# The order of a fused spectral-filter and expert kernel: x turned ahead of the previous tile's second product, a rank product timed by VectorE's count, and later landing times for loads

## The chip, the cores and the metric

The kernel runs on one core of one Trainium2 chip. The metric is the device time of one execution in microseconds (us); the time before is 1613.07 us, the median of three runs (1609.99 to 1613.96). PE is TensorE, DVE is VectorE, ACT is ScalarE, POOL is GpSimd, SP is SyncE, whose queue issues the direct DMAs.

## What is computed

The input x is (8, 2496, 256), all data float32. Each of the 8 batches is filtered along its sequence, and the filtered tokens then go through a mixture of 8 experts, one expert per token:

```python
X = np.fft.rfft(x, axis=1)
y = np.fft.irfft(X * (filt_r + 1j * filt_i), n=2496, axis=1)   # per batch and channel
x = y.reshape(19968, 256)
logits = x @ w_gate                                            # 8 experts
expert = argmax(logits); gate = softmax(logits)[expert]
out[token] = gate * (relu(x[token] @ w1[expert]) @ w2[expert]) # hidden width 1024
```

## The kernel before

**Two halves, one instruction stream.** The filter half takes the transform of length 2496 as 39 x 64: four matrix products a batch, called stages a, b, c and d, with the result of a stored in DRAM (zd) and read again for b, and that of c stored (ud) and read again for d. Stage b also multiplies by the filter on DVE (lines 358 to 362). After stage d the tokens are transposed (turn_y), the logits formed, and `route` ranks the tokens of each expert and scatters them to a list in DRAM with indirect DMAs on POOL (line 606). `tile_map` then works out, on rows of 8 to some 160 numbers, which expert and which row of the list each tile takes (lines 625 to 676).

The expert half works through that list in tiles of 512, 256 and, at the end, 128 rows. One tile i has these parts:

- `turn_x` (T below): 8 transposes for a 512-row tile on PE (line 736), copies to xT, copies of the token numbers and gates to idt and gts on DVE (lines 730, 731; three buffers), and four subtractions on POOL that form `sums` (lines 742 to 745);
- two `half`s (H): the product with w1, the hidden width split in two. Tiles of 512 rows and 256-row tiles of the last batch save one product in eight by combining quarters (`hidden_by_quarters`): seven products in all, each four matmuls in the profile; the third product is the first to need `sums`. Each also needs `wsum`, four sums over the weights on POOL (lines 752 to 755). DVE adds the parts (line 779), ACT copies and applies relu (lines 788, 783). Other tiles use `hidden` (line 816);
- `result` once per 128 rows (R, four for a 512-row tile): 16 matmuls in the profile with w2 (line 833), scaling by the gate to ys on ACT or DVE (lines 837, 838), and an indirect DMA on POOL that writes the 128 rows of the output (line 839).

**What sets the order.** The program is written out at build time by a planner: the loop at the end of the kernel keeps a modelled clock `now`, and takes either the next filter step (`STEPS`) or the next expert step (the generator `experts`). The order on PE, DVE, ACT and SP is that of the program; on POOL the framework chooses it. The planner's rules that the change touches:

- `more_loads` issues the filter half's loads and writes their modelled landing to `lands`. If the next filter step's load counts as not yet landed (`late_in`), an expert step may go first even without credit.
- `prefetch` does the same for x and the weights of the expert half; `due` asks whether their modelled landing is past.
- `side` runs the steps of `route` and `tile_map`, up to four between two planner steps. For each bare `yield` it adds 0.3 us to `free["v"]`, the planner's count of when DVE is free. `either` uses `free["v"]` to place a copy on DVE or ACT. A `yield "wait"` costs one of the four calls and nothing else.
- In `route` sixteen such waits, thus about four planner steps, stand between the one-hot tile `oe` (line 526, DVE) and the rank products that read it (lines 537, 538, PE).
- `experts` orders a tile's parts. In the steady state, with everything due, the order on PE is ... R(i-1), T(i+1), H(2i+1), H(2i+2), R(i), T(i+2) ...: the next tile's first half already stands ahead of the last tile's second product, and T stands behind it.

Of the kernel before, what the change touches and what calls it, by code (L numbers as in the profile page):

```python
# [118 lines left out]
def kernel(  # L119
# [92 lines left out]
    now = [0.0]  # L212
    free = {"v": 0.0, "s": 0.0, "p": 0.0}
# [284 lines left out]
    def route(b, g):  # L498
        t0 = 8 * g
        w = min(8, NG - t0)  # L500
        lg = lgs[b][:, t0:t0 + w]
        sh3 = (TP, w, E)
        she = (TP, E, w)

        def small(name, *shape, dt=F32, tag=None, rows=TP):
            n = int(np.prod(shape))
            full = sb.tile([rows, 8 * n // w if w in shape else n], dt, tag=tag or name, name=name, bufs=1)[:, :n]
            return full.rearrange("p (a b) -> p a b", a=shape[0]) if len(shape) == 2 else full

        mx = small("mx", w)  # L510
        nc.vector.tensor_reduce(mx, lg, axis=AX.X, op=ALU.max)
        oh = small("oh", w, E)
        ex = small("ex", w, E)
        nc.vector.tensor_tensor(oh, lg, mx[:, :, None].to_broadcast(sh3), op=ALU.is_ge)
        yield
        nc.vector.tensor_tensor(ex, lg, mx[:, :, None].to_broadcast(sh3), op=ALU.subtract)
        nc.scalar.activation(ex, ex, AF.Exp)
        nc.vector.tensor_tensor(oh, oh, em8[:TP, None, :].to_broadcast(sh3), op=ALU.mult)
        yield
        idx = small("idx", w)  # L520
        nc.vector.tensor_reduce(idx, oh, axis=AX.X, op=ALU.min)

        nc.vector.tensor_tensor(idx, idx, vld[:, t0:t0 + w], op=ALU.mult)
        yield
        oe = small("oe", E, w)
        nc.vector.tensor_tensor(
            oe, idx[:, None, :].to_broadcast(she), em8[:TP, :, None].to_broadcast(she), op=ALU.is_equal
        )
        sd = small("sd", w)
        nc.vector.tensor_reduce(sd, ex, axis=AX.X, op=ALU.add)  # L530
        yield

        for _ in range(16):
            yield "wait"
        rk = psr.tile([P, 2, E * NG], F32, tag="rk", name="rk")
        oef = oe.rearrange("p e t -> p (e t)")
        mm(rk[:TP, 0, :E * w], lhsT=tri, rhs=oef, start=True, stop=True)
        mm(rk[:, 1, :E * w], lhsT=ones, rhs=oef, start=True, stop=True)
        rks = sb.tile([P, 2, 8 * E], F32, tag="rks", name="rks", bufs=1)
        nc.vector.tensor_copy(rks[:TP, 0, :E * w], rk[:TP, 0, :E * w])  # L540
        nc.vector.tensor_copy(rks[:, 1, :E * w], rk[:, 1, :E * w])
        nc.vector.tensor_scalar(sd, in0=sd, scalar1=1e-9, scalar2=None, op0=ALU.add)
        nc.vector.reciprocal(sd, sd)
        yield
        yos = [outs.pop(("o", b, c)) for c in range(2 * g, min(2 * g + 2, len(CH)))]
        for c, yo in enumerate(yos):
            n = min(4, w - 4 * c)
            sh8 = (TP, n, 8)
            nc.vector.tensor_scalar(
                yo.bitcast(I32)[:, :n, D:D + 8], in0=ids0[:, t0 + 4 * c:t0 + 4 * c + n, None].to_broadcast(sh8),  # L550
                scalar1=float(b * S), scalar2=None, op0=ALU.add,
            )
            nc.vector.tensor_copy(yo[:, :n, D + 8:], sd[:, 4 * c:4 * c + n, None].to_broadcast(sh8))
            yield
        run = small("run", E, w, rows=P)
        runf = run.rearrange("p e t -> p (e t)")
        nc.vector.tensor_tensor_scan(
            runf, segs[w], rks[:, 1, :E * w], 0.0, op0=ALU.mult, op1=ALU.add
        )
        yield  # L560

        pos = small("pos", E, w)
        posf = pos.rearrange("p e t -> p (e t)")
        nc.vector.tensor_tensor(posf, runf[:TP], rks[:TP, 1, :E * w], op=ALU.subtract)
        nc.vector.tensor_tensor(posf, posf, rks[:TP, 0, :E * w], op=ALU.add)
        yield
        bs = sb.tile([TP, E], F32, tag="bs", name="bs", bufs=1)
        nc.vector.tensor_tensor(bs, cnt[:TP], eoff[:TP], op=ALU.add)
        nc.vector.tensor_tensor(pos, pos, bs[:, :, None].to_broadcast(she), op=ALU.add)
        yield  # L570
        nc.vector.tensor_tensor(pos, pos, oe, op=ALU.mult)
        rowf = small("rowf", w)
        nc.vector.tensor_reduce(rowf, pos.rearrange("p e t -> p t e"), axis=AX.X, op=ALU.add)
        yield
        row = sb.tile([TP, 8], U32, tag="row", name="row", bufs=2)[:, :w]
        nc.vector.tensor_copy(row, rowf)
        nc.vector.tensor_tensor(cnt, cnt, run[:, :, w - 1], op=ALU.add)
        yield
        rows = []
        for t in range(w):  # L580
            m = N1 if t0 + t == NG - 1 else TP
            rows.append((row[:m, t:t + 1], yos[t // 4][:m, t % 4, :]))
        pool(now[0] + 2.0, 0)
        for at, what in rows:
            scatter(b, at, what)
            yield "pool"
        held_y[0] -= len(yos)
        if t0 + w == NG:
            rows_at[b] = free["p"] + 4.0
# [30 lines left out]
    def tile_map(b, rows, n, last):  # L620
# [6 lines left out]
        nc.vector.tensor_scalar(  # L627
            av_i, in0=av_i, scalar1=rows.bit_length() - 1, scalar2=None, op0=ALU.arith_shift_right
        )
        yield  # L630
        nc.vector.tensor_copy(av, av_i)
        nc.vector.tensor_tensor_scan(end, one, av, 0.0, op0=ALU.mult, op1=ALU.add)

        base = pools["moe"].tile([1, E], F32, name="base", bufs=1)
        add = pools["moe"].tile([1, E], F32, name="add", bufs=1)
        nc.vector.tensor_tensor(base, done, eoff[0:1, :], op=ALU.add)
        yield
        nc.vector.tensor_scalar(add, in0=av, scalar1=-float(rows), scalar2=None, op0=ALU.mult)
        nc.vector.tensor_tensor(add, add, base, op=ALU.subtract)
        nc.vector.tensor_tensor(add[:, :E - 1], add[:, :E - 1], base[:, 1:], op=ALU.add)  # L640
        yield
        most = max(m for group in GROUPS for _, m in group)
        tau = pools["moe"].tile([1, most], F32, tag="tau", name="tau", bufs=1)[:, :n]
        past = pools["moe"].tile([1, most, E - 1], F32, tag="past", name="past", bufs=1)[:, :n]
# [1 line left out]
        nc.vector.tensor_tensor(  # L646
            past, tau0[:, :n, None].to_broadcast(she), end[:, None, :E - 1].to_broadcast(she), op=ALU.is_ge
        )
        yield
        ef = pools["moe"].tile([1, most], F32, tag="ef", name="ef", bufs=1)[:, :n]  # L650
        erow = pools["moe"].tile([1, n], I32, tag=f"erow{n}", name="erow", bufs=2)
        nc.vector.tensor_reduce(ef, past, axis=AX.X, op=ALU.add)
        nc.vector.tensor_copy(erow, ef)
        nc.vector.tensor_tensor(past, past, add[:, None, :E - 1].to_broadcast(she), op=ALU.mult)
        yield
        rf = pools["moe"].tile([1, most], F32, tag="rf", name="rf", bufs=1)[:, :n]
        rrow = pools["moe"].tile([1, n], I32, tag=f"rrow{n}", name="rrow", bufs=2)
        nc.vector.tensor_reduce(rf, past, axis=AX.X, op=ALU.add)
# [6 lines left out]
            nc.vector.tensor_scalar(rrow, in0=rf, scalar1=stop[:, 0:1], scalar2=None, op0=ALU.min)  # L665
        else:
            nc.vector.tensor_copy(rrow, rf)
        yield
        if not last:

            take = pools["moe"].tile([1, E], F32, name="take", bufs=1)
            nc.vector.tensor_tensor(take, av, end, op=ALU.subtract)
            nc.vector.tensor_scalar(take, in0=take, scalar1=float(n), scalar2=0.0, op0=ALU.add, op1=ALU.max)
            nc.vector.tensor_tensor(take, take, av, op=ALU.min)
            nc.vector.tensor_scalar(take, in0=take, scalar1=float(rows), scalar2=None, op0=ALU.mult)
            nc.vector.tensor_tensor(done, done, take, op=ALU.add)
            yield
        work.extend((rows // P, erow[0:1, i:i + 1], rrow[0:1, i:i + 1], b) for i in range(n))


# [232 lines left out]
    def more_loads():  # L913

        while todo and len(ins) < NIN:
            kind, b, c = todo[0]
            if kind != "x" and ({"z": "a", "u": "c"}[kind], b) not in stored:
                return
            todo.pop(0)
            {"x": load_x, "z": load_z, "u": load_u}[kind](b, c)  # L920
            lands[kind, b, c] = now[0] + 6.0

    def after(b):
        for rows, n in GROUPS[b]:
# [5 lines left out]
    def side():  # L930

        while sides and not (held[0] == "pool" and free["p"] > now[0] + 1.5):
            try:
                held[0] = next(sides[0])

                free["v"] = max(free["v"], now[0]) + (0.3 if held[0] is None else 0.0)
                return
            except StopIteration:
                sides.pop(0)
                held[0] = None  # L940
# [24 lines left out]
    def experts():  # L965
# [4 lines left out]
        def turned(i):  # L970
            if used["x"] == i:
                yield lambda: turn_x(i), 0.22 * TILES[i][0], ("x", i)
                used["x"] += 1
# [19 lines left out]
        def due(what, i):  # L993
            return when.get((what, i), now[0] + 1.0) <= now[0]

        for i in range(NT):
            yield from turned(i)
            if used["w1"] == 2 * i:
                yield from half(2 * i)
            if due("x", i + 1):  # L1000
                yield from turned(i + 1)
            yield from half(2 * i + 1)
            if used["x"] == i + 2 and due("w1", 2 * i + 2):
                yield from half(2 * i + 2)
            for j in range(TILES[i][0]):
                yield lambda: result(i, j), 3.42, ("w2", 2 * i + 1)
            hs.pop(i), idt.pop(i), gts.pop(i), w2t.pop(2 * i, None), w2t.pop(2 * i + 1, None)
            used["w2"] += 2

    def share():  # L1010

# [74 lines left out]
```

## Time and profile before

| | |
|---|---|
| time, median of 3 | 1613.07 us |
| span of the profiled execution | 1615.9 us |
| PE busy | 1530.9 us, 95% of the span, 7624 matmuls |
| DVE busy | 753.2 us, 47% |
| ACT busy | 519.6 us, 32% |
| POOL busy | 671.9 us, 42% |
| matmuls with w2 in the 4- and 2-block tiles (line 833) | 500.7 us, 2240 of them, 381 ns each by the profile |
| DMA | 287.54 MB, 178 GB/s over the span |
| mean granted PE clock | 0.979 |

Reading it: PE's spans overlap, since a matmul starts before the one ahead of it has ended; sixteen matmuls of 128x256 that the profile gives as 381 ns each take 3.45 us in a row. PE's idle time is what counts here, and the list of PE's waits gives it by the instruction that waited and what it waited for. From 1100 us on only the expert half is left; before that the two halves are mixed; the first 200 us have little or no expert work to mix in.

### The profile page before, as it was taken

The page shows a single profiled execution, that of the slowest core. Times are in us where ns is not written, and L with a number is a line of the kernel's source. Part 1 is how long each engine was busy: PE and PEld are TensorE (multiplying, and loading weights), DVE is VectorE, ACT ScalarE, POOL GpSimd, SP SyncE. Part 2 cuts the span into 40 slices and gives each one's busy share as a digit, 9 for nine tenths or more (in the row PEclk, how much of TensorE's full clock was granted, in tenths as well). Part 3 has the DMA queues.
Part 4 walks back from the last instruction along what each step waited for, and adds up shares of the span by engine and source line. Part 5 has one row for each costly group of instructions (what it writes and reads, how often), then busy time and mean ns, then how long its engine had stood idle before and what let it go on. Part 6 is the DMA issues. An engine that isn't in the chain of part 4 may idle for free. (4 is left out here: it accounts for less than half of the span.)

```text
span 1615.9 us, 24022 instructions
## 1 busy us (share of the span) xinstructions
PE 1530.9 (95%) x7624; PEld 1213.0 (75%) x7624; DVE 753.2 (47%) x1938; ACT 519.6 (32%) x1059; POOL 671.9 (42%) x817
## 2 busy tenths in 40 slices
PE   7989877999999999999999898999998999999998
PEld 6534546677678778886788687787887888999997
DVE  4677664344755664356555354365342334420000
ACT  4434332333333233222333232223231222233433
POOL 4132224314534644354445545554445446631111
PEclk9999998999999999999999999999999999999999
DMA  8679866697865494356544623352343547676561
GB/s 240 170 201 297 270 215 222 210 279 226 245 203 179 146 283 144 99 160 174 165 128 127 193 93 118 111 156 92 117 161 137 165 133 253 191 240 177 173 188 36
DMA packets 119280, 287.54 MB, mean 178 GB/s; under 512 B 17587, under 2 KB 58812, under 8 KB 119157
## 3 DMA queue, kind: packets, MB, share of 16 engines
q1 hardware_dynamic: 99941, 242.69, 50.0%
q0 software_dynamic: 19216, 43.33, 7.8%
q8 instruction: 62, 1.02, 0.3%
q14 instruction: 61, 0.50, 0.1%
HBM read 205.95 MB, written 80.90 MB: 178 GB/s over the span
## 5 line engine op out<-in xcount | busy, mean ns | idle before, releaser
L833 PE MATMUL bank<-w2t,hT 128*128 128x256 f32 x2240 | 500.7, 381 | 0.0
L833 PEld LDWEIGHTS bank<-w2t,hT 128*128 128x128 f32 x2240 | 424.8, 191 | 73.3 <-issue 16.7
L839 POOL DMA_INDIRECT out_dram<-ys,idt x163 | 163.0, 1000 | 551.9 <-ACT ys L838 205.9
L779 DVE TENSOR_TENSOR hT<-bank,hT 128x512 f32<-128x512 f32 (+1 forms) x504 | 299.3, 627 | 147.0 <-PE bank L775 65.2
L606 POOL DMA_INDIRECT rows<-yo,row x176 | 174.7, 993 | 197.9 <-issue 63.2
L783 ACT ACTIVATE hT<-hT 128x1024 f32<-128x1024 f32 (+1 forms) x144 | 132.4, 956 | 337.7 <-DVE hT L779 330.9
L775 PE MATMUL bank<-sums,wsum 128*128 128x256 f32 (+1 forms) x864 | 189.6, 367 | 28.8 <-POOL sums L743 18.3
L838 ACT ACTIVATE ys<-bank,gts 128x256 f32<-128x256 f32 x160 | 75.7, 473 | 409.9 <-PE bank L833 333.1
L775 PEld LDWEIGHTS bank<-sums,wsum 128*128 128x128 f32 x864 | 152.6, 195 | 61.0 <-POOL sums L743 20.5
L227 DVE COPY xT<-bank 128x128 f32<-128x128 f32 (+2 forms) x55 | 25.9, 471 | 308.1 <-PE bank L736 267.8
L816 PE MATMUL bank<-xT,w1t 128*128 128x128 f32 (+1 forms) x928 | 132.9, 298 | 0.0
L816 PEld LDWEIGHTS bank<-xT,w1t 128*128 128x128 f32 x928 | 120.3, 192 | 11.5 <-issue 5.9
L775 PE MATMUL bank<-xT,w1t 128*128 128x256 f32 (+1 forms) x576 | 123.8, 358 | 0.6 <-ACT hT L788 0.4
L775 PEld LDWEIGHTS bank<-xT,w1t 128*128 128x128 f32 x576 | 99.0, 191 | 15.4 <-issue 3.0
L752 POOL TENSOR_TENSOR wsum<-w1t 128x256 f32<-128x256 f32 x73 | 53.9, 738 | 112.2 <-PE bank L775 97.6
L358 DVE TENSOR_TENSOR ys<-bank,ht 128x512 f32<-128x512 f32 x80 | 54.9, 687 | 86.3 <-PE bank L351 60.4
L372 PE MATMUL bank<-ys,tcs 128*128 128x512 f32 x140 | 74.9, 617 | 12.4 <-DVE ys L362 7.9
L822 ACT ACTIVATE hT<-bank 128x128 f32<-128x128 f32 (+1 forms) x229 | 67.9, 299 | 57.2 <-PE bank L816 45.4
L833 PE MATMUL bank<-w2s,hT 128*128 x368 | 83.2, 379 | 0.0
L391 PE MATMUL bank<-fin,tds 120*117 120x512 f32 x140 | 68.2, 608 | 8.3 <-DMA fin<-ud 7.4
L337 PE MATMUL bank<-fin,tas 117*120 117x512 f32 x154 | 75.5, 609 | 0.0
L351 PE MATMUL bank<-fin,tbs 128*128 128x512 f32 x140 | 75.0, 619 | 0.1
(149 smaller groups left out, 1757.9 us busy)
## 6 DMA issues: line engine op xcount, KB each, us to landing
w1t<-in_moe_w_dram SPq DMA_DIRECT2D x130, 512.0 KB
w2t<-in_moe_w_dram SPq DMA_DIRECT2D x84, 512.0 KB
fin<-in_x_dram SPq DMA_DIRECT2D x40, 512.0 KB
fin<-zd SPq DMA_DIRECT2D x70, 256.0 KB
ud<-uo SPq DMA_DIRECT2D x70, 256.0 KB
zd<-zo SPq DMA_DIRECT2D x35, 480.0 KB
fin<-ud SPq DMA_DIRECT2D x35, 480.0 KB
xg<-rows SPq DMA_DIRECT2D x28, 544.0 KB
```

Source lines behind the costliest of these rows:

```text
L337: mm(p[:TK, :], lhsT=tas, rhs=xt[:TP, j:j + 2, :], start=True, stop=True)
L351: mm(p, lhsT=tbs, rhs=zi[:, j:j + 2, :], start=True, stop=True)
L372: mm(p, lhsT=tcs, rhs=ys, start=True, stop=True)
L391: mm(p[:TP, :], lhsT=tds, rhs=ui[:TK, j:j + 2, :], start=True, stop=True)
L606: sc = nc.gpsimd.indirect_dma_start(out=rowsd, out_offset=bass.IndirectOffsetOnAxis(ap=at, axis=0), in_=what, in_offset=None,)
L775: mm(q[:, v], lhsT=left[:, v * P:(v + 1) * P], rhs=right, start=True, stop=True)
L779: nc.vector.tensor_tensor(o, q, a, op=ALU.add)
L783: nc.scalar.activation(o.rearrange("p v r c -> p v (r c)"), q.rearrange("p v r c -> p v (r c)"), AF.Relu)
L816: mm(p[:, :m], lhsT=w1t[2 * i + g][:, dh, fh, v * P:(v + 1) * P], rhs=xts[i][:, dh, :m], start=(dh == 0), stop=(dh == DH - 1))
L833: mm(p[:, :D], lhsT=hs[i][k % 4 // 2][:, k // 4, k % 2, j * P:(j + 1) * P], rhs=w2, start=(k == 0), stop=(k == FT - 1))
L838: lambda: nc.scalar.activation(ys, p[:, :D], AF.Copy, scale=gate))
L839: nc.gpsimd.indirect_dma_start(out=out, out_offset=bass.IndirectOffsetOnAxis(ap=idt[i].bitcast(U32)[:, j, :], axis=0), in_=ys, in_offset=None,
```

## The change

Four edits to the planner; the arithmetic stays as it is.

1. `experts`: T of the tile after next stands ahead of R, so that the order becomes ... H(2i), T(i+1), R(i-1), H(2i+1), H(2i+2), T(i+2), R(i) ... It is meant to give POOL the time of R to form `sums`. If w1 or x of the next tile isn't due, R goes first as before.
2. `route`: in place of the sixteen waits, the rank products wait until the modelled clock has passed the planner's count of VectorE plus 1.0 us.
3. `route` and `tile_map`: each yield carries a number, and `free["v"]` grows by 0.15 us times that number rather than by 0.3 us. Most numbers are 2; others are 1, 3, 4 and 5.
4. `more_loads`: loads count as landed 10 rather than 6 us after their issue.

```diff
@@ route
-        yield
+        yield 2
 ...
-        for _ in range(16):
+        due = free["v"] + 1.0
+        while now[0] < due:
             yield "wait"
         rk = psr.tile([P, 2, E * NG], F32, tag="rk", name="rk")
 ...
         nc.vector.reciprocal(sd, sd)
-        yield
+        yield 4
@@ tile_map: yields of 3, 3, 3, 2, 3, 4 and 5
@@ more_loads
-            lands[kind, b, c] = now[0] + 6.0
+            lands[kind, b, c] = now[0] + 10.0
@@ side
-                free["v"] = max(free["v"], now[0]) + (0.3 if held[0] is None else 0.0)
+                if isinstance(held[0], int):
+
+                    free["v"] = max(free["v"], now[0]) + 0.15 * held[0]
                 return
@@ experts
-        for i in range(NT):
-            yield from turned(i)
-            if used["w1"] == 2 * i:
-                yield from half(2 * i)
-            if due("x", i + 1):
-                yield from turned(i + 1)
-            yield from half(2 * i + 1)
-            if used["x"] == i + 2 and due("w1", 2 * i + 2):
-                yield from half(2 * i + 2)
+        def results(i):
             for j in range(TILES[i][0]):
                 yield lambda: result(i, j), 3.42, ("w2", 2 * i + 1)
             hs.pop(i), idt.pop(i), gts.pop(i), w2t.pop(2 * i, None), w2t.pop(2 * i + 1, None)
             used["w2"] += 2
+
+        for i in range(NT):
+            ahead = i > 0 and (used["x"] > i or due("x", i)) and due("w1", 2 * i)
+            if i > 0 and not ahead:
+                yield from results(i - 1)
+            yield from turned(i)
+            yield from half(2 * i)
+            if i + 1 < NT and due("x", i + 1):
+                yield from turned(i + 1)
+            if ahead:
+                yield from results(i - 1)
+            yield from half(2 * i + 1)
+        yield from results(NT - 1)
```

More of the change, by code (lines that the diff above doesn't have):

```diff
@@ L518, in route @@
         nc.vector.tensor_tensor(oh, oh, em8[:TP, None, :].to_broadcast(sh3), op=ALU.mult)
-        yield
+        yield 2
         idx = small("idx", w)
@@ L523, in route @@
         nc.vector.tensor_tensor(idx, idx, vld[:, t0:t0 + w], op=ALU.mult)
-        yield
+        yield 2
         oe = small("oe", E, w)
@@ L530, in route @@
         nc.vector.tensor_reduce(sd, ex, axis=AX.X, op=ALU.add)
-        yield
-        for _ in range(16):
+        yield 2
+        due = free["v"] + 1.0
+        while now[0] < due:
             yield "wait"
@@ L543, in route @@
         nc.vector.reciprocal(sd, sd)
-        yield
+        yield 4
         yos = [outs.pop(("o", b, c)) for c in range(2 * g, min(2 * g + 2, len(CH)))]
@@ L553, in route @@
             nc.vector.tensor_copy(yo[:, :n, D + 8:], sd[:, 4 * c:4 * c + n, None].to_broadcast(sh8))
-            yield
+            yield 2
         run = small("run", E, w, rows=P)
@@ L559, in route @@
         )
-        yield
+        yield 1
         pos = small("pos", E, w)
@@ L565, in route @@
         nc.vector.tensor_tensor(posf, posf, rks[:TP, 0, :E * w], op=ALU.add)
-        yield
+        yield 2
         bs = sb.tile([TP, E], F32, tag="bs", name="bs", bufs=1)
@@ L569, in route @@
         nc.vector.tensor_tensor(pos, pos, bs[:, :, None].to_broadcast(she), op=ALU.add)
-        yield
+        yield 2
         nc.vector.tensor_tensor(pos, pos, oe, op=ALU.mult)
@@ L573, in route @@
         nc.vector.tensor_reduce(rowf, pos.rearrange("p e t -> p t e"), axis=AX.X, op=ALU.add)
-        yield
+        yield 2
         row = sb.tile([TP, 8], U32, tag="row", name="row", bufs=2)[:, :w]
@@ L577, in route @@
         nc.vector.tensor_tensor(cnt, cnt, run[:, :, w - 1], op=ALU.add)
-        yield
+        yield 2
         rows = []
@@ L629, in tile_map @@
         )
-        yield
+        yield 3
         nc.vector.tensor_copy(av, av_i)
@@ L636, in tile_map @@
         nc.vector.tensor_tensor(base, done, eoff[0:1, :], op=ALU.add)
-        yield
+        yield 3
         nc.vector.tensor_scalar(add, in0=av, scalar1=-float(rows), scalar2=None, op0=ALU.mult)
@@ L640, in tile_map @@
         nc.vector.tensor_tensor(add[:, :E - 1], add[:, :E - 1], base[:, 1:], op=ALU.add)
-        yield
+        yield 3
         most = max(m for group in GROUPS for _, m in group)
@@ L648, in tile_map @@
         )
-        yield
+        yield 2
         ef = pools["moe"].tile([1, most], F32, tag="ef", name="ef", bufs=1)[:, :n]
@@ L654, in tile_map @@
         nc.vector.tensor_tensor(past, past, add[:, None, :E - 1].to_broadcast(she), op=ALU.mult)
-        yield
+        yield 3
         rf = pools["moe"].tile([1, most], F32, tag="rf", name="rf", bufs=1)[:, :n]
@@ L667, in tile_map @@
             nc.vector.tensor_copy(rrow, rf)
-        yield
+        yield 4
         if not last:
@@ L676, in tile_map @@
             nc.vector.tensor_tensor(done, done, take, op=ALU.add)
-            yield
+            yield 5
         work.extend((rows // P, erow[0:1, i:i + 1], rrow[0:1, i:i + 1], b) for i in range(n))
```

## The prediction

> **What bounds the kernel now.** I began with the page's busy times.
>
> ```profile
> PE 1530.9 (95%) x7624; PEld 1213.0 (75%) x7624; DVE 753.2 (47%) x1938; ACT 519.6 (32%) x1059; POOL 671.9 (42%) x817
> ```
>
> PE is the bound, and the change takes no matmul away. So all it can win is PE's idle time, 1615.9 - 1530.9 = 85.0 us, and what a slower clock costs after it. The last 18.7 us of the span (from the last matmul of the chain that ended last, at 1597.2 us) is the drain of the last outputs, which no edit touches. That leaves 66 us. The list of PE's waits says whose they are.
>
> ```profile
> engine line waited for: us in total, times, longest us
> PE bank L775 <- POOL sums L743: 18.3, 6, 7.0
> PE bank L372 <- DVE ys L362: 7.9, 6, 2.8
> PE bank L391 <- DMA fin<-ud: 7.4, 2, 5.7
> PE rk L537 <- DVE oe L526: 5.9, 1, 5.9
> PE bank L775 <- DVE hT L779: 5.5, 2, 3.8
> PE bank L413 <- DMA fin<-in_x_dram: 5.4, 1, 5.4
> PE bank L775 <- POOL wsum L753: 4.8, 1, 4.8
> ```
>
> Three rows meet an edit: sums (edit 1), fin<-ud (edit 4), rk (edits 2 and 3). For the largest I read the timeline of PE, then of POOL, around its longest wait.
>
> ```profile
> 1220.57 1.04 PE L736 MATMUL bank<-ident,xg 128*128 128x128 f32 x8
> 1221.44 1.89 PE L775 MATMUL bank<-xT,w1t 128*128 128x256 f32 x8
> ...
> 1227.83 1.89 PE L775 MATMUL bank<-xT,w1t 128*128 128x256 f32 x8
> 1236.70 4.45 PE L775 MATMUL bank<-sums,wsum 128*128 128x256 f32 x12 [6.99 <-POOL sums L743]
> 1240.99 1.03 PE L775 MATMUL bank<-sums,w1t 128*128 128x256 f32 x4
> ```
> ```profile
> 1226.98 0.99 POOL L839 DMA_INDIRECT out_dram<-ys,idt  x1 [4.22 <-ACT hT L788]
> 1234.11 0.98 POOL L839 DMA_INDIRECT out_dram<-ys,idt  x1 [6.14 <-DVE hT L779]
> 1235.11 0.74 POOL L742 TENSOR_TENSOR sums<-xT 128x256 f32<-128x256 f32 x1
> 1235.93 0.72 POOL L743 TENSOR_TENSOR sums<-xT,sums 128x256 f32<-128x256 f32 x1
> ```
>
> The reader is to see a queue, not a slow sum. A sum takes 0.7 us. It stands behind the last of R's four output DMAs on POOL, and each of those starts only after the one before has landed: the chain that ended last puts DMA and waiting of 6 us between 1227.97 and 1233.94 us. Where the DMA engines are less loaded the gap is 2.2 us:
>
> ```profile
> 1329.32 0.98 POOL L839 DMA_INDIRECT out_dram<-ys,idt  x1 [4.18 <-DMA out_dram<-ys,idt]
> 1332.53 0.98 POOL L839 DMA_INDIRECT out_dram<-ys,idt  x1 [2.23 <-DMA out_dram<-ys,idt]
> ```
>
> **What the skill says.** "DMA: Bandwidth & Descriptors", Anatomy of one DMA, gives a DMA issued from GpSimd a fixed part of about 2.0 us, mostly completion: the 2.23 us agrees, the 6 us shows that it grows. "TensorE: Matmul & The Clock Gate", Architectural detail, calls ACT, DVE and GpSimd strict first-in-first-out queues: the sums behind the output DMA agree. The same page, What's actually happening, says that PE falls to half its clock after about 3.4 us of idleness and needs as long to recover. Here the twelve matmuls after the wait took 1240.99 - 1236.70 = 4.29 us to the next group, against 2.59 us in an undisturbed tile (1259.13 to 1261.72): 1.7 us more. So a long wait costs more than its length.
>
> **Edit 1, T ahead of R.** No instruction is added or removed; 8 transposes (0.87 us) move ahead of 64 matmuls (13.8 us). Before, from the end of T to the first use of sums there is one half and two products, 6.05 + 1.73 = 7.8 us, in which POOL must finish R's last output DMA and two sums. Afterwards R lies between too: 7.8 + 13.8 = 21.6 us, and the sums go to POOL ahead of R's four DMAs. Even four slow output DMAs of the tile before, at 7 us each, fit. All six waits should go: 18.3 us. After the waits of 7.0 us (1236.7) and 5.1 us (1000.9) the first twelve matmuls lost 1.7 and 1.8 us to the clock, so 3.5 us more. The waits of 2.9 and of about 1 us show no such loss. Edit 1: -21.8 us.
>
> What is queued behind the moved T? On DVE, the idt copy (line 730) waits until the outputs of two tiles back have landed, since idt has three buffers: 60.7 us in 23 times in the view of the output tensor, 2.6 us each. It keeps its place in DVE's order, since R puts nothing on DVE while ys is on ACT. But xT's copies and the next adds now follow it at once. The first PE work to need them is H(2i+1) after R, 13.8 us later. So 2.6 us, even 7, is hidden behind R. PSUM: with seven banks, R's first bank is that of the third product of the half before, whose add ran within 2 us; I cost it at nothing. The 128-row tiles at the end use no sums: nothing.
>
> **Edits 2 and 3, the rank and the count.** The one long wait for oe, 5.9 us, ends at 238.07 us. DVE was busy without a gap from 226.2 to 243.7 us: two runs of tile_map (22 small instructions each, 3.5 us), stage b and route. The new numbers charge a tile_map run (3+3+3+2+3+4+5) x 0.15 = 3.45 us, where seven bare yields charged 2.1, so the planner will hold this rank back. But what PE takes instead ends in a product of stage c, whose filter multiplies stood in the same DVE queue until 240.9 us. Most of the wait moves to that product. What can be won is DVE's idle time afterwards, 2.8 us (at 246.50), and part of the 2.7 us that the slow clock cost there. I take -3; bounds 0 and -8.6 (5.9 + 2.7).
>
> The other side: where DVE has little counted, the rank comes about 1.2 + 1.0 = 2.2 modelled us after oe was queued instead of four planner steps, which beside expert work are 0.85 to 3.4 us each. In an undisturbed tile DVE's adds end 1.7 us after PE's (1271.2 against 1269.5 us), and route's eight instructions to oe and sd take 1.5 us: 3.2 us, so PE may wait up to 1 us at some of the 24 ranks. Bounds 0 and 24; I take +4. Behind a waiting rank stands all of PE.
>
> **Edit 4, landing at 10.** The wait of 5.7 us for fin<-ud came at 891.4 to 897.1 us, with a whole R (13.8 us) at hand that could have gone first. Four more modelled us leave about 1.7, too short for the clock: -4.0, and -2.5 for the clock (the stage d product and the next took 3.53 and 1.59 us to the next group, instead of 1.71 and 0.86). The other, 1.8 us at 131 us, has no expert work to put in: nothing. Edit 4: -6.5. Bounds 0 and -8.2.
>
> **Sum.** -21.8 - 3 + 4 - 6.5 = -27.3 us. The mix of the two halves before 1000 us will be another one, and its waits with no edit of their own (stage c on DVE, 7.9 us; hT, 5.5; logits, 3.2) will fall elsewhere. I add 2 for that, no more, as I have no reason for a sign: about -25 us, 1588 us.
>
> **The rivals.**
> - *Only edit 1 pays.* Stage c and the ranks take back what edits 2 to 4 win, since DVE, 62 to 70% busy between 100 and 200 us and between 400 and 600, has little room: +9 for the waits at ranks and in stage c against -21.8: 1600 us. For it: the waits for DVE are many and short. Chance 0.22.
> - *More than the sum.* The better count also places the copies better and half of PE's waits for DVE (7.9, 5.9, 5.5 and 3.2, so 22.5 us) go, with 2 us of clock: 1588 - 13 = 1575 us. Against it: only one rank waited. Chance 0.18.
> - *No change.* The POOL queue stays the bound, another instruction waits in it: 1612 us. Chance 0.06.
> - *Slower.* The idt wait takes the place of the sums wait. If half of its 60.7 us reached PE, +30 - 21.8 = +8: 1621 us; the same comes from 24 ranks at 1 us with a few long waits in the filter half. For it: DVE is a strict queue and the wait now stands directly ahead of xT. Against it: 13.8 us of R hide it. Chance 0.13.
>
> **How the numbers follow.** The forecast, 1588, has 0.41. Faster is the forecast with the first two rivals: 0.81; same 0.06; slower 0.13. The low end takes in the second rival with some spread, 1570; the high end goes to 1611, past the first rival and just short of no change, so that the slower case and part of no change are left out.
>
> **What would show it.** In the profile after: no row of PE waiting for sums, or under 2 us; the order T, R, H, H on PE from 1000 us on; POOL's sums ahead of the output DMAs of the R beside them; from there to the last matmul no clock below full. The wait for fin<-ud under 3 us. The wait for rk shorter than 5.9 us at its longest, with small ones beside it. I would be wrong if PE waits for xT or for hT right after R (then idt is the cause), or if the waits at lines 537, 480 and 372 together grow by over 10 us.

## The result, and the profile after

The changed kernel took 1586.33 us (median of four runs, 1583.86 to 1590.51), the kernel before 1611.53 us beside it (1608.00 to 1613.96). The ratio is 0.9848, with a 95% interval of 0.9815 to 0.9881: 25 us faster, where 1588 us was forecast. The profiled execution spans 1582.1 us instead of 1615.9; the one before took 1618.45 us by the device time, 7 us over 1611.53, so the profiles differ by more than the medians do.

The busy times on the page, after:

```profile
PE 1519.9 (96%) x7624; PEld 1207.6 (76%) x7624; DVE 748.4 (47%) x1923; ACT 524.1 (33%) x1074; POOL 669.5 (42%) x817
```

PE has as many matmuls as before. Of the 33.8 us between the two spans, 11.0 are shorter busy time, with a mean granted clock of 0.989 instead of 0.979, and 22.8 are idle time (85.0 to 62.2 us). The list of PE's waits after, columns as in the prediction (total, times, longest):

```profile
PE bank L737 <- DMA xg<-rows: 9.6, 2, 5.6
PE bank L776 <- POOL wsum L754: 8.3, 2, 5.1
PE bank L372 <- DVE ys L362: 7.9, 7, 3.6
...
PE bank L834 <- DMA w2t<-in_moe_w_dram: 4.3, 2, 3.4
...
PE bank L391 <- DMA fin<-ud: 2.2, 1, 2.2
PE bank L776 <- POOL sums L744: 1.8, 2, 1.5
...
PE rk L538 <- ACT ls L227: 1.0, 2, 0.5
```

The wait for sums fell from 18.3 to 1.8 us, that for fin<-ud at line 391 from 7.4 to 2.2 (with 1.5 more at line 395, where there was none), that for oe at the rank from 5.9 to nothing; 1.0 us at the rank is put down to an ACT copy (ls) instead. The row of xg and that of wsum have grown (3.1 to 9.6, 4.8 to 8.3), and w2t is new.

The timeline of PE after, one tile of 512 rows (start, length, instruction):

```profile
1226.35 1.89 PE L776 MATMUL bank<-xT,w1t 128*128 128x256 f32 x8
1228.08 2.75 PE L776 MATMUL bank<-sums,wsum 128*128 128x256 f32 x12
1230.67 1.03 PE L776 MATMUL bank<-sums,w1t 128*128 128x256 f32 x4
1231.53 1.03 PE L776 MATMUL bank<-xT,wsum 128*128 128x256 f32 x4
1232.39 1.04 PE L737 MATMUL bank<-ident,xg 128*128 128x128 f32 x8
1233.27 13.98 PE L834 MATMUL bank<-w2t,hT 128*128 128x256 f32 x64
1247.08 1.89 PE L776 MATMUL bank<-xT,w1t 128*128 128x256 f32 x8
```

T (line 737) now stands ahead of R (line 834). The same tile on POOL:

```profile
1236.12 0.73 POOL L743 TENSOR_TENSOR sums<-xT 128x256 f32<-128x256 f32 x1 [0.55 <-ACT xT L227]
...
1239.18 1.00 POOL L840 DMA_INDIRECT out_dram<-ys,idt  x1 [0.15 <-issue]
1242.66 0.98 POOL L840 DMA_INDIRECT out_dram<-ys,idt  x1 [2.48 <-DMA out_dram<-ys,idt]
1245.87 0.98 POOL L840 DMA_INDIRECT out_dram<-ys,idt  x1 [2.23 <-DMA out_dram<-ys,idt]
1251.90 0.98 POOL L840 DMA_INDIRECT out_dram<-ys,idt  x1 [5.06 <-DMA out_dram<-ys,idt]
```

The sums begin at 1236.12 us, ahead of the tile's output DMAs. These still wait for each other, for 2.2 to 5.06 us, but nothing that PE needs soon stands behind them.

### The profile page after: what moved, and what is told of

The parts are those of the page before. It is cut to its first block, busy times and chain, and to the rows that moved or that the text cites. A ratio compares the mean times of both kernels' runs of the same rounds, so it can differ in the third digit from the quotient of the medians.

```text
span 1582.1 us, 24007 instructions
## 1 busy us (share of the span) xinstructions
PE 1519.9 (96%) x7624; PEld 1207.6 (76%) x7624; DVE 748.4 (47%) x1923; ACT 524.1 (33%) x1074; POOL 669.5 (42%) x817
## 4 chain that ended last, share of the span: by engine, by line
PE 71%; DMA 11%; issue 8%; DVE 4%; POOL 4%; ACT 1%; POOLq 0%; SPq 0%; ACTq 0%; DVEq 0%
PE bank L834 28%; PE bank L776 20%; DMA out_dram<-ys,idt 6%; PE bank L391 4%; PE bank L351 3%; PE bank L372 3%; PE bank L337 3%; PE bank L817 3%; DMA zd<-zo 2%; PE bank L466 2%; PE bank L737 2%; PE lt L480 1%; DVE hT L780 1%; DMA fin<-ud 1%; PE bank L413 1%
## 5 line engine op out<-in xcount | busy, mean ns | idle before, releaser
L817 PEld LDWEIGHTS bank<-xT,w1t 128*128 128x128 f32 x928 | 123.0, 193 | 18.0 <-issue 8.2
L776 PEld LDWEIGHTS bank<-xT,w1t 128*128 128x128 f32 x576 | 100.7, 190 | 16.2 <-issue 4.1
L731 DVE COPY idt<-xg 128x4 int32<-128x4 int32 (+2 forms) x65 | 19.3, 297 | 176.2 <-DMA out_dram<-ys,idt 143.0
L834 PE MATMUL bank<-w2s,hT 128*128 x368 | 83.2, 379 | 0.0
L834 PEld LDWEIGHTS bank<-w2s,hT 128*128 128x128 f32 x368 | 68.1, 190 | 8.3
```

Source lines behind the costliest of these rows:

```text
L776: mm(q[:, v], lhsT=left[:, v * P:(v + 1) * P], rhs=right, start=True, stop=True)
L817: mm(p[:, :m], lhsT=w1t[2 * i + g][:, dh, fh, v * P:(v + 1) * P], rhs=xts[i][:, dh, :m], start=(dh == 0), stop=(dh == DH - 1))
L834: mm(p[:, :D], lhsT=hs[i][k % 4 // 2][:, k // 4, k % 2, j * P:(j + 1) * P], rhs=w2, start=(k == 0), stop=(k == FT - 1))
```

## The experiments

Comparisons differ here by as much as an edit is worth: the changed kernel itself took 1586.3 us in the first one, of which the record doesn't name the chip, and 1603.8 us in experiment 9. Each ratio below is to the kernel before on the same chip, and only runs of one chip are set against each other closely. Runs 1 to 4 shared a chip, 5 to 8 another, 9 to 12 a third. A gain in us that stands beside a ratio is worked out from the ratio. Experiments named by edit use the numbers of the section on the change.

**1. Edit 1 alone.** The kernel before with the new `experts`:

```diff
+            ahead = i > 0 and (used["x"] > i or due("x", i)) and due("w1", 2 * i)
 ...
+            if ahead:
+                yield from results(i - 1)
             yield from half(2 * i + 1)
```

> Edit 1 alone on the kernel before (T ahead of R; waits, count and landing times as before). Theory (sums stand behind the output DMAs in POOL's queue; the new order gives them the time of R): the six PE waits for sums, 18.3 us, go with 3.5 us of slow clock, so about 1590 us, ratio 0.986, and no wait of PE for sums above 2 us. Rival (the gain comes from edits 2 to 4 and from the filter half falling differently; a shift in the order only moves the waits): above 1603 us, ratio 0.995 or more, with other waits of PE in place of those for sums.

Measured: 1596.13 us against 1615.73, ratio 0.9887 (0.9860 to 0.9914), by which it is 18 us faster. PE's waits in this run:

```profile
PE rk L537 <- DVE oe L526: 5.9, 1, 5.9
...
PE bank L391 <- DMA fin<-ud: 3.2, 2, 1.8
...
PE bank L775 <- POOL sums L743: 2.6, 3, 1.3
```

Three waits for sums are left, 2.6 us, and none is longer than 1.3, as expected of each. PE's matmuls on sums and wsum took 186.2 us instead of 189.6, 3.4 us less, where the prediction had put the slow clock at 3.5. PE's busy time in all fell by 8.8 us; the rest of that isn't traced. The rank's wait is untouched. So this edit alone gives 18 us, where the whole change gave 25 in the first comparison and 14 in experiment 9.

**2. Edits 2 and 3 alone.**

```diff
-        for _ in range(16):
+        due = free["v"] + 1.0
+        while now[0] < due:
             yield "wait"
```
and the numbered yields.

> Edits 2 and 3 alone (the rank waits for the count of VectorE, the yields carry numbers; old order, landing at 6). Theory: -3 for the long wait at the rank, +4 for small waits at other ranks: 1612 us, ratio 1.000 within 0.003; the wait of 5.9 us at the rank moves to stage c. Rival (the better count pays by itself): 1600 us, ratio 0.993, with PE's waits for VectorE in all halved from 22 us.

Measured: 1627.66 us, ratio 1.0075 (1.0047 to 1.0102), 12 us slower. Both expectations fail. The waits and, from the groups of instructions, the row of the matmuls on sums and wsum (count, busy us, mean ns, idle before and what it waited for):

```profile
PE bank L776 <- POOL sums L744: 18.9, 6, 5.7
...
PE bank L737 <- issue: 6.7, 1, 6.7
...
PE rk L538 <- DVE oe L526: 1.2, 3, 0.5
```
```profile
L776 PE MATMUL bank<-sums,wsum 128*128 128x256 f32 (+1 forms) x864 | 200.3, 380 | 29.6 <-POOL sums L744 18.9 <-POOL wsum L754 7.3 <-DVE hT L780 2.3
```

The same row of the kernel before:

```profile
L775 PE MATMUL bank<-sums,wsum 128*128 128x256 f32 (+1 forms) x864 | 189.6, 367 | 28.8 <-POOL sums L743 18.3 <-DVE hT L779 5.5 <-POOL wsum L753 4.8
```

The ranks did what they were meant to: 5.9 us became 1.2. PE's idle time in all went from 85.0 to 86.5 us, so the loss is not in waits. PE's busy time rose by 10.7 us (1530.9 to 1541.6), and this one row rose by 10.7 us (189.6 to 200.3). It is the row that comes after the waits for sums and wsum. Set against undisturbed groups of as many matmuls (2.75 us for twelve, 1.89 for eight, 1.04 for four), the groups that follow a wait for sums lost 9.9 us by my estimate from the two timelines, against 3.5 in the kernel before, and those after a wait for wsum 4.3 against 2.1. An example from this run's timeline, twelve matmuls that take 2.75 us undisturbed:

```profile
1234.20 2.75 PE L776 MATMUL bank<-sums,wsum 128*128 128x256 f32 x12
1246.07 5.49 PE L776 MATMUL bank<-sums,wsum 128*128 128x256 f32 x12 [5.66 <-POOL sums L744]
```

So a wait of 5.66 us cost 8.4. Why the waits of nearly the same total met longer slow stretches here isn't shown, and experiment 4 shows that the loss doesn't rest on this row alone. There is also the first x tile: T comes at 180.93 us instead of 164.89, after a wait of 6.7 us (experiment 8).

**3. Edit 4 alone.** One number:

```diff
-            lands[kind, b, c] = now[0] + 6.0
+            lands[kind, b, c] = now[0] + 10.0
```

> Edit 4 alone (loads of the filter half count as landed 10 us after issue; all else as before). Theory: the wait for fin<-ud falls from 5.7 us to under 2 us and its clock loss goes: -6.5 us, 1605 us, ratio 0.996. Rival (the mix of the halves changes with it and the waits fall elsewhere): within 0.002 of 1, or slower, with other waits of 5 us or more before 1000 us.

Measured: 1611.49 us, ratio 0.9971 (0.9955 to 0.9986), 4.7 us faster. The longest wait for fin<-ud is down from 5.7 to 2.1 us, though there are four now, 5.7 us together:

```profile
PE bank L391 <- DMA fin<-ud: 5.7, 4, 2.1
```

The long wait is gone as expected, though not to under 2 us, and part of it comes back as short ones. The total of these waits fell by only 1.7 us and PE's idle time is 84.9 us, as before (85.0), so the profile doesn't show where 4.7 us come from. The interval takes in the theory's 0.996 and the rival's 0.998 alike.

**4. Edits 2, 3 and 4 without edit 1.** The changed kernel with the old `experts`.

> The changed kernel with the old order of the expert half (edits 2, 3 and 4 without edit 1). Theory: the sum of the small terms, -3 + 4 - 6.5 = -5.5 us, 1606 us, ratio 0.9965; PE's waits for sums stay near 18 us. Rival (edits 2 to 4 carry the gain): 1592 us or less, ratio 0.988.

Measured: 1619.90 us, ratio 1.0018 (1.0002 to 1.0034). The three small edits don't carry the gain; PE's waits for sums are 17.2 us at line 744 and 1.6 at 745. 1.0018 lies near the product of experiments 2 and 3, 1.0046, below it. This run is experiment 3 with edits 2 and 3 added, on the same chip, and is 8.4 us slower, with intervals that don't meet. Yet the row of matmuls on sums and wsum takes as long in both, here and then in experiment 3:

```profile
L776 PE MATMUL bank<-sums,wsum 128*128 128x256 f32 (+1 forms) x864 | 193.5, 371 | 32.0 <-POOL sums L744 17.2 <-POOL wsum L754 7.8 <-DVE yw L360 3.3
L775 PE MATMUL bank<-sums,wsum 128*128 128x256 f32 (+1 forms) x864 | 193.5, 372 | 30.5 <-POOL sums L743 19.4 <-DVE hT L779 6.6 <-POOL wsum L753 4.4
```

What grew here are waits: for ys at stage c 13.1 us against 8.1, for the rows of x 7.8 against 4.9, for wsum 7.8 against 4.4, while the 5.9 us at the rank went. So edits 2 and 3 cost about 10 us in the old order in two settings, and the profiles don't put the cost in the same place twice; that of experiment 3 is of an execution 5 us over the median, so this pair shows only 4.2 of the 8.4 us.

**5. Edits 1 and 4 without 2 and 3.** The changed kernel with sixteen waits and bare yields.

> The changed kernel without edits 2 and 3 (sixteen waits, bare yields; new order, landing at 10). If the terms add up as measured alone (order 0.9887, landing 0.9971): ratio 0.986, as far down as the changed kernel itself (0.9848), so that edits 2 and 3 bring nothing there. Theory of the prediction (+1 for edits 2 and 3): the same within 0.002. Rival (edits 2 and 3 cost 12 us by themselves, as in their own run, whatever the order): 0.978, faster than the changed kernel by 10 us or more.

Measured: 1590.51 us against 1611.28, ratio 0.9875 (0.9858 to 0.9892). This is far from the rival's 0.978. But that number took the first comparison's 0.9848 for the changed kernel, which was not on this chip, so this run alone doesn't tell what edits 2 and 3 cost with the new order; experiments 6 and 10 say more.

**6. Edits 1, 2 and 3 without 4.** Landing at 6 again in the changed kernel.

> The changed kernel with loads counted as landed 6 us after issue. If edit 4 is worth the same here as alone: 0.0029 slower than the changed kernel, ratio 0.988, and a wait for fin<-ud of 3 us or more. If edit 4 pays for the late start that edit 2 brings: 0.994, the sum of order and rank alone (0.9887 and 1.0075).

Measured: 1590.58 us, ratio 0.9870 (0.9853 to 0.9886). Order alone and rank alone would multiply to 0.9961, and 0.994 was the expectation for that case: the loss of experiment 2 is gone when the order is new. It also equals experiment 5 on the same chip, so with edit 1 in place edits 2 and 3 are worth what edit 4 is worth, which is no loss unless edit 4 loses too. It fits that with the new order there are hardly any waits for sums to be followed by slow matmuls: their row takes 187.4 us here, not 200.3. After experiment 4 this can be only part of the reason. The wait for fin<-ud at line 391 is 5.9 us in four pieces, none over 2.3, where 3 us or more was expected.

**7. The output DMAs unchained, old order.** The kernel before; the output DMAs write rows of their own and are declared free of each other, as the code does already for the scatters of line 606:

```diff
-        nc.gpsimd.indirect_dma_start(
+        wr = nc.gpsimd.indirect_dma_start(
             out=out,
 ...
+        tc.declare_no_dep(wr.ins, group="outs", reason="rows of their own")
+        tc.add_to_no_dep_group("outs", wr.ins)
```

> The kernel before, in its old order, with the output DMAs declared free of each other (they write rows of their own), so that one no longer waits for the landing of the one ahead. Theory (sums are late because they stand behind a chain of output DMAs that wait for each other's landing): PE's waits for sums fall from 18.3 us to under 5 us with the order untouched, ratio about 0.988 as with edit 1 alone. Rival (the sums are late for ys, for ACT or for the place of T, whatever the chain): waits for sums of 12 us or more, ratio above 0.995.

Measured: 1585.88 us against 1611.28, ratio 0.9844 (0.9829 to 0.9860), 25 us faster. POOL's timeline at the place where the kernel before had its longest wait, after the same eight pad scatters:

```profile
1202.04 0.99 POOL L839 DMA_INDIRECT out_dram<-ys,idt  x1 [0.31 <-issue]
1203.34 0.99 POOL L839 DMA_INDIRECT out_dram<-ys,idt  x1 [0.30 <-issue]
1204.63 0.98 POOL L839 DMA_INDIRECT out_dram<-ys,idt  x1 [0.30 <-issue]
1205.63 0.74 POOL L742 TENSOR_TENSOR sums<-xT 128x256 f32<-128x256 f32 x1
```

Output DMAs follow each other at 1.3 us and the sums come at once. PE's waits for sums are one of 0.3 us, with T still behind R. That shows the cause: with POOL's instructions and the place of T as before, the waits go when the chain goes in which each output DMA waits for the landing of the one ahead, with the sums behind them. The gain is larger than the expected 0.988; what it brings beyond the sums isn't shown.

**8. The first three ranks as before.** In the profile after, the first 200 us had become slower: PE was busy 83.2 us between 100 and 200 us, against 87.6 before, and the first T waited for its rows:

```profile
143.75 0.31 PE L538 MATMUL rk<-oe,tri 117*117 117x48 f32 x2
...
178.33 1.08 PE L737 MATMUL bank<-ident,xg 128*128 128x128 f32 x4 [5.57 <-DMA xg<-rows]
```

The third rank's oe was ready at 132.8 us; the rank came 11 us later, 4.7 later than in the kernel before (139.08), the scatters at 150.3 instead of 143.3, and the load of the first x tile at 172.0 instead of 160.4. The edit:

```diff
+        if b == 0:
+            for _ in range(16):
+                yield "wait"
         due = free["v"] + 1.0
-        while now[0] < due:
+        while b > 0 and now[0] < due:
             yield "wait"
```

> The changed kernel, but the three ranks of batch 0 stand behind sixteen waits as before; the others by the count. Theory formed from the profile after (in the first 200 us the count runs ahead of VectorE, holds the third rank back by 5 us, and with it the scatters and the first x tile, for which PE then waits 5.6 us): the scatters of the third group begin near 143 us instead of 150, PE's idle time between 100 and 200 us falls from 16.8 to about 12.4 us as in the kernel before, ratio about 0.981. Rival (the late first tile is bought back later, since the filter half runs ahead meanwhile): the same as the changed kernel, 0.985, with the idle time elsewhere.

Measured: 1580.30 us against 1611.28, ratio 0.9788 (0.9766 to 0.9811). The first part of the theory holds:

```profile
141.32 0.31 PE L541 MATMUL rk<-oe,tri 117*117 117x48 f32 x2
...
166.08 0.60 PE L740 MATMUL bank<-ident,xg 128*128 128x128 f32 x4
```

The scatters begin at 145.5 us, the first T comes at 166.08, 12 us earlier and without a wait. But the idle time between 100 and 200 us is 15.8 us, not 12.4: waits for loads and for stage c came in place of the one for rows. What changed in that stage is the mean granted clock, 0.97 instead of 0.90. So it is shown that the count held the rank back and what followed from it; that this is what makes the run faster is not, the more as the changed kernel was not on this chip. Experiment 5 speaks against it: there the first T comes at 163.56 us, as early as here, and the time is that of experiment 6, where it comes at 178.61. The kernel after had made the delay good soon: PE was busy 273.0 us between 100 and 400 us, against 268.5 before. Experiments 5 and 6 differ in edit 4 too, but everything here fits the rival, in which the late tile is bought back. What makes run 8 some 10 us faster than 5 and 6 stays open.

**9 to 12, on one chip.** The changed kernel as it is; with sixteen waits at every rank but the numbered yields; with the edits of experiments 7 and 8 together; and the last with the old order of the expert half.

> The changed kernel as it is, beside the next three for a closer interval: 0.985, within 0.002.

> Edits 1, 3 and 4 without 2: the yields carry numbers, the rank stands behind sixteen waits. It tells the count from the wait. If the count places the copies better by itself: 0.979, as with the first ranks as before. If what pays is the rank that waits for the count after batch 0: 0.9875, as with edits 1 and 4 alone (0.9875). In both, no late first tile: PE busy 84 us or more between 100 and 200 us, and the wait of 4 to 6 us for oe at one rank stays in the second case.

> The changed kernel with the first three ranks behind sixteen waits and the output DMAs free of each other. The changed order already gives the sums the time of R, so only the small rest is left: waits for sums of 2.7 us and the idt copies. Theory: 0.977, 2 to 3 us better than with the chain (0.9788). Rival (unchaining is worth 25 us whatever the order, as in its own run): 0.965.

> The same with the old order of the expert half (T behind R). Theory (the new order and the unchained outputs remove one and the same wait): within 0.003 of the new order with unchained outputs, so about 0.977 to 0.980. Rival (the order brings something of its own beside the sums): 0.984 or more.

| run | us | ratio | interval | PE's waits for sums, us |
|---|---|---|---|---|
| 9, the changed kernel | 1603.77 | 0.9910 | 0.9874 to 0.9946 | 2.8 |
| 10, sixteen waits, numbered yields | 1601.46 | 0.9906 | 0.9872 to 0.9940 | 3.2 |
| 11, unchained, first ranks as before | 1589.09 | 0.9827 | 0.9793 to 0.9860 | none |
| 12, the same with the old order | 1588.94 | 0.9836 | 0.9795 to 0.9877 | 0.9 |

Run 9 missed its expectation: 14 us faster than before here, 25 us in the first comparison. Of the 22.1 us between the two profiles of the changed kernel, 12.0 are PE's busy time (1531.9 instead of 1519.9), with a mean granted clock of 0.984 instead of 0.989; among the waits, those for VectorE grew with the same instructions: hT 4.2 instead of 1.0 us at line 776, and one of 3.6 us for yw at stage c. Why isn't shown.

Run 10 equals run 9, so the rank that waits for the count brings nothing that can be measured once the other edits are there. It keeps the wait of 5.9 us at one rank, and its first T comes at 164.83 us, not at 179.72 as in run 9 (PE busy 87.3 us between 100 and 200 us, against 82.7). The two may cancel; but as in experiments 5 and 6 the early tile brings no gain that can be seen.

Runs 11 and 12 differ by 0.0009, well inside their intervals: with the outputs unchained the order is worth nothing more that can be measured. The two remove one and the same wait. The absolute expectations (0.977 to 0.980) were too low here, like that of run 9. Run 11 is 14.7 us faster than the changed kernel on the same chip, and their intervals don't meet. How much of it is the first ranks and how much the chain, these runs don't separate.

## Why the prediction was right, and where it was not

**The bound.** The prediction put the last matmul at 1597.2 us and a drain of 18.7 us after it. That was misread: the chain of waits turns there to the output DMAs, but PE goes on. The timeline of the kernel before ends so:

```profile
1606.06 3.62 PE L833 MATMUL bank<-w2s,hT 128*128 x16
```

The drain is 1615.9 - 1609.7 = 6.2 us. PE had 79 us of idle time ahead of it, not 66, which is what the list of waits adds up to (78.3). No term of the sum used the 66, so the forecast wasn't hurt.

**Edit 1, -21.8 forecast, -18 measured alone.** The mechanism was right at each step: the sums wait behind a chain of output DMAs (experiment 7), T ahead of R takes them out (experiment 1), and the row of matmuls after such waits takes 3.4 us less. All six waits were to go, and 2.6 us of them stay; the forecast lies within the interval of 14 to 23 us all the same. The Trainium skill's page "TensorE: Matmul & The Clock Gate" (What's actually happening) gave the reason to price a wait above its length, and the runs agree: 1.7 us more in the kernel before, up to 2.7 in experiment 2. But the 3.4 us of idleness that this section gives, and that the prediction took over, are no safe line between waits with a loss and without. In experiment 2 a wait of 2.59 us was followed by a loss of 1.8, where one of 2.88 us in the kernel before had lost 0.1:

```profile
1077.80 4.54 PE L776 MATMUL bank<-sums,wsum 128*128 128x256 f32 x12 [2.59 <-POOL sums L744]
```

**The waiting idt copy.** The prediction costed it at nothing, with R above it. On DVE it grew and became 7.5 us at its longest:

```profile
DVE idt L731 <- DMA out_dram<-ys,idt: 143.0, 25, 7.5
```

In the list of PE's waits after there is none for xT. The rival that ended slower rested on this wait, and it fell: the 13.8 us of R are enough to hide 7.5.

**Edits 2 and 3, -3 and +4 forecast, 12 us slower measured alone.** This step failed. It looked for the cost at the ranks and put +4 there; the waits at ranks are 2.2 us in experiment 2 and 1.0 after. It said that the planner would hold the rank of 238 us back and did not ask which others it would hold: the third, which came at 143.75 us in the kernel after instead of 139.08, and with it the scatters and the first x tile. That delay is shown, but the runs don't show that it costs time. The loss stood elsewhere: in experiment 2 in slower matmuls on sums and wsum, in experiment 4 by its profile not there, so its cause is open. Edits 2 and 3 lost 8 to 12 us in the old order (experiments 2, and 4 against 3) and nothing that can be seen in the new one (6 against 5; edit 2 in 10 against 9). That is why the total was not hurt, and the prediction had not counted on it: this part was luck.

**Edit 4, -6.5 forecast, -4.7 measured alone.** The wait it aimed at was the right one: it fell from 5.7 us to 2.1 at its longest. It became short waits that the prediction had not counted, and that PE's idle time did not fall leaves the rest of the mechanism unshown.

**The sum.** -27.3 + 2 = -25 forecast, -25 measured in the first comparison and -14 in experiment 9. The terms alone give 0.9887 x 1.0075 x 0.9971 = 0.9932, or -11 us, so they don't simply add: the 12 us of edits 2 and 3 shrink when edit 1 is there. That the sum fell so close was in part luck, as one term was wrong by 11 us and the two comparisons of the changed kernel differ by as much.

**What was to be seen.** The order T, R, H, H, the sums ahead of the output DMAs, no wait for sums over 2 us, the longest wait for fin<-ud under 3 us: all there. The waits at the ranks, logits and stage c together went from 22 us to 9, where growth by 10 would have refuted. The clock was to be full from 1000 us to the last matmul, and its mean is 1.00 in each stretch from there to 1576 us; it is lower (0.86) in the last 6 us alone, where no matmul runs. Not foreseen: the later first tile (xg, 5.6 us), more waits for wsum, and w2t (4.3 us, near 1391 us). The last comes with the new order as long as the outputs are chained: it is 1.5 to 4.8 us in experiments 1, 5, 6, 8, 9 and 10, and at most 0.3 in every run with the old order and in experiment 11. I did not pursue how.

## What to carry to other kernels

When an engine waits for a short operation, look at what stands ahead of that operation in its queue and what that in turn waits for; here 0.7 us sums stood behind DMAs that waited for each other, and each of two cures, moving the work ahead of the queue or cutting the false chain, took the waits away, while both together brought nothing measurable over the second alone. When a wait is retimed by an estimate, ask which other waits the same rule retimes, and don't take a delay that the profile shows at one place for a cost in the end. Price a wait by its length and by the slow matmuls that may follow it, test an edit together with the others as well as alone, and compare small edits on one chip only.

## What the runs showed of the hardware that I had not expected

- The changed kernel took 1586.3 us in one comparison and 1603.8 in another, 1.1% apart, while the kernel before differed by 0.4% beside it (1611.5 and 1618.0). On the three chips on record the kernel before took 1615.7, 1611.3 and 1618.0 us.
- Output DMAs of 128 rows, issued on GpSimd, landed in 2.1 to 10.3 us, with a median of 2.5 (the view of the output tensor after). The Trainium skill's page "DMA: Bandwidth & Descriptors" (Anatomy of one DMA) gives about 2.0 as the fixed part, which the lower end agrees with. How busy the DMA engines were goes with the gap between two of them: in the kernel before their mean share was 0.73 and 0.70 around the wait of 6.14 us (1222 to 1228 and 1228 to 1234 us) and 0.11 during the one of 2.23 us (1329 to 1332.5 us); after, it was 0.78 over the wait of 5.06 us (1246 to 1252 us) and 0.12 over one of 2.23 (1243 to 1246 us).
- A wait of 5.66 us cost 2.7 us more in one run (5.49 us for matmuls that take 2.75), one of 6.99 us cost 1.7 in another, one of 2.59 us 1.8 and one of 2.88 us 0.1, so the penalty doesn't follow the length of the wait.
